# A subtraction one group earlier, a third chunk loaded into the result tile, and a reordered opening

## The chip, the cores and the metric

One core of one Trainium2 chip runs the whole program. The metric is the device time of one execution in microseconds (us); lower is better. Engines are named as in the profile: PE (TensorE matrix multiply), PEld (its weight load), DVE (VectorE), ACT (ScalarE), POOL (GpSimd), SP (the queue from which most transfers are issued).

## What is computed

The input is x (4 sequences of 4224 tokens with 192 channels). Three layers follow each other:

```python
# 1: a causal convolution of 7 taps, one softmax of the weights per head
out = np.einsum('hk,bskhg->bshg', w, x_unf)
# 2: rotation, mixing over all tokens, channel matrix
theta = x @ w_theta
zr = x * cos(theta);  zi = x * sin(theta)
y = einsum('ts,bsd->btd', w_tok_r, zr) + einsum('ts,bsd->btd', w_tok_i, zi)
u = x + y
x = u + np.maximum(u @ w_ch, 0.0)
# 3: low-rank token mixing (rank 32) and a two-layer channel network (192 -> 768 -> 192)
```

(In the reference z is formed from the convolved x; the kernel takes its rotated copy from the same theta product.) `w_tok_r` and `w_tok_i` are 4224 x 4224 each and stored in 64-bit floats, so they are most of what is loaded (308 MB are read in all).

## The kernel before

The mixing of layer 2 fills about three quarters of the run. Its result stays in one on-chip tile `yt` of six rows (`yt[:, j, :]`, j = 0 to 5: two pairs of sequences with three row blocks each) by 4224 token columns. Source tokens come in 33 blocks of 128. A **step** g (`mix_steps`, line 41) is one or two source blocks against one or two chunks of 512 target columns; each step has six **groups**, one per row j, and a group is 12 matmuls of 128x512 in the usual case (real and imaginary weights, and three products each: high by high, high by low, low by high, since each number is split into a rounded high part and the rest). `products` (line 764) issues them, `evict` (line 779) adds the sum from PSUM (the accumulator memory, four buffers `acc`) to `yt`. For the first source block evict copies on ACT (line 786) or, where told, on DVE (788); later it adds on DVE (784).

The weights of a step are two **pieces**, a = 2g (real) and b = 2g + 1 (imaginary). A piece goes through a chain: a transfer from SP into a raw buffer (`load_w`, line 394; a ring of two buffers `wraw`), unpacking of the 64-bit floats to 32 bits (`unpack_low` on ACT, line 278; `unpack_scale`, line 283 on ACT or 285 on DVE; `unpack_sign` 292 and `unpack_shift` 297 on DVE; the opening calls the last one "join"), the high part (ACT cast, line 703, into a ring of four tiles `w`), and the low part (subtraction, line 708, on DVE or POOL). The end of that subtraction frees the raw buffer and issues the transfer of the piece that follows in the ring (line 717). In the job lists below (piece, 0) is low and scale, (piece, 1) sign and shift, (piece, 2) the high part, (piece, 3) the subtraction.

`split_plan` (line 97) hands these jobs out by hand: list n of a step runs after the eviction of its group n. In a step of `TAILS` a **tail** (line 871: 128 more columns, with weights of their own) comes after group 3; lists 6 and 7 run within it, and lists 4 and 5 after groups 4 and 5. There are 15 such steps: the fourth step of each stage of eight steps from the third stage on (14 stages; stages 3 to 16, every 141.5 us) and step 10 in the second stage. There c is the first piece of the step after next.

Meanwhile the next source blocks are made in **units** (`prep_stages`, line 493): convolution (on DVE, lines 525 and 527, seven taps in two parts each, or on PE with diagonal matrices, line 537, then a copy by ACT, line 545), high and low parts (551; 573, 577, 581), theta (PE, lines 590 to 594), the reduction of the angle (617), sine and cosine, the rotation (635 and 638, "rot"), and high and low part of z (649 on ACT, "z_hi"; 652, "z_lo"), and `x_add` (658, on POOL), which adds the convolved x to `yt`. `unit_slots` plans them by group; the jobs of a list come before the unit's operations of the same group. In a tail step of the fourth stage and later, rot 1 and z_hi come at group 4, the first low/high casts of another unit (551) at group 5, its low parts (573 to 581) after group 0 of the next step, and its theta after group 2 of the next step.

The first three steps are written out by hand as the word list `OPENING` (line 65), which `open_mix` (795) executes in order: `W4.low` is a part of piece 4, `g1_3.0a` half a group of step 1 with row 3, `eg1_3.0` its eviction, `u0`, `u1`, `A`, `B` the first four units, `B.pc3` tap 3 of unit B on PE, `B.conva3` and `B.convb3` would be its two parts on DVE; `@dve` and `@pool` choose the engine. Each engine keeps the order of the words that are its own. Pieces 0 and 1 start in the ring, 2 and 3 in spare columns of `yt`; pieces 4 and 5 take the ring's buffers after pieces 0 and 1, and 6 and 7 after 4 and 5.

Of the kernel before, what the change touches and what calls it, by code (L numbers as in the profile page):

```python
# [12 lines left out]
I32 = mybir.dt.int32  # L13
# [5 lines left out]
P = 128  # L19
B, S, D = 4, 4224, 192  # L20
# [44 lines left out]
OPENING = """  # L65
    dg0.0 dg1.0 dg1.5 SL dg0.2 u0.pc0 dg1.1 dg1.6 dg0.1 dg0.5 dg1.4@act dg0.6@act dg0.4@act dg1.3@act dg0.3 dg1.2@act
    u0.pc1 u0.pc2 u0.pc3 u0.pc4 T.low u0.pc5 T.scale@dve T.sign W0.low u0.pc6 T.join T.t3 W1.scale T.t1 u1.pc0 W1.low
    u0.xhi2 T.t2@pool u1.pc1 W0.scale@dve T.t4@pool W0.sign W0.join u1.pc2 u0.xhi0@dve u0.xlo0 u0.xlo2 u0.xhi1 u1.pc3
    W1.sign u0.xcp u0.xlo1 W2.scale@dve W2.low W1.join u0.theta u1.pc4 W3.scale u0.turn0 W2.sign u0.turn1 W3.low
    W2.join u1.pc5 u1.pc6 u0.red0 u0.red1 u0.red2 u1.xhi2@dve u1.xhi0 W0.hi W1.hi u1.xhi1@dve u0.abs u1.xlo2 A.pc0  # L70
    u1.xlo0 u0.cos W0.lo@pool A.pc1 u1.xlo1 u0.rot0 W1.lo@pool A.pc2 u1.xcp A.pc3 A.pc4 A.pc5 A.pc6 u0.sin W3.sign
    u0.zhi0 A.xhi1 A.xhi2 A.xlo1 A.xlo2 A.xhi0 u0.zlo0@pool A.xcp u0.rot1 u1.theta u1.turn0 u0.zhi1 g0_0.0a u1.turn1
    u0.zlo1@pool W2.hi W3.join A.xlo0 u1.red0 g0_1.0a g0_2.0a A.theta g0_0.0 g0_1.0 u1.red1 u1.red2 W3.hi u1.abs
    eg0_0.0 W2.lo W3.lo u1.sin g0_2.0 A.turn0 eg0_1.0@dve eg0_2.0@dve u1.cos u1.rot0 A.xadd g1_0.0a u1.rot1 g1_0.1a
    g1_0.0 W4.low g1_0.1 u1.zhi0 g1_1.0a eg1_0.1 A.turn1@dve g1_1.1a u1.zhi1 eg1_0.0 u1.zlo0 g1_1.0 A.red0
    u1.zlo1@pool g1_1.1 g1_2.0a W5.low g1_2.1a g1_2.0 g1_2.1 B.pc0 eg1_1.1 eg1_1.0 B.pc1 W4.scale A.red1 g0_3.0a
    A.red2 g0_3.0 B.pc2 B.pc3 g0_4.0a eg1_2.0 eg1_2.1 A.abs g0_4.0 B.pc4 B.pc5 eg0_3.0 eg0_4.0 g0_5.0a g0_5.0 B.pc6
    B.xcp B.xhi2 B.xhi1 A.sin g1_3.0a W5.scale g1_3.0 B.xlo2 B.xhi0 g1_3.1a eg0_5.0 B.xlo1 B.xlo0 g1_3.1 g1_4.0a
    W4.sign W4.join eg1_3.0 W4.hi g1_4.0 W5.sign W5.join eg1_3.1 A.cos g1_4.1a W4.lo W5.hi A.rot0 g1_4.1 g1_5.0a
    g1_5.0 g1_5.1a W5.lo eg1_4.0 g1_5.1 eg1_4.1 A.zhi0 g2_0.0a g2_0.0 B.theta eg1_5.0 A.zlo0 W6.scale@dve W6.low  # L80
    eg1_5.1 A.rot1 B.turn0 W6.sign g2_1.0a g2_1.0 W6.join eg2_0.0 A.zhi1 B.turn1 W7.scale g2_2.0a g2_2.0 W7.low W6.hi
    eg2_1.0 B.red0 B.red1 B.red2 W7.sign eg2_2.0 g2_3.0a B.xadd B.abs W7.join A.zlo1 W6.lo g2_3.0 B.cos B.sin W7.hi
    B.rot0 g2_4.0a g2_4.0 eg2_3.0 B.zhi0 B.zlo0 W7.lo@pool eg2_4.0@dve B.rot1 W8.scale@dve W8.low B.zhi1 W8.sign
    g2_5.0a g2_5.0 B.zlo1 W8.join eg2_5.0 u1.xadd@dve u0.xadd@dve
""".split()
IDLE = 13
OPENED = 3
# [9 lines left out]
def split_plan():  # L97

    def following(g):
        return ("t", g + 1) if g + 1 in TAILS else 2 * (g + 2)  # L100

    plan = {}
    for g in range(OPENED, STARTS[-1]):
        a, b, c = 2 * (g + 1), 2 * (g + 1) + 1, following(g)
        if g in TAILS:
            t = ("t", g)
            jobs = [[(t, 2)], [(t, 3), (a, 0)], [(a, 1)], [(a, 2)], [(b, 2)], [(b, 3), (c, 0), (c, 1)]]
            jobs += [[(a, 3), (b, 0)], [(b, 1)]]
# [144 lines left out]
def mix_kernel(ctx, tc, xT, wcv, wth, wtok, wch, uu, vv, w1, w2, outT):  # L253
    nc = tc.nc
# [81 lines left out]
    with tc.manual_schedule():  # L336
# [27 lines left out]
        pieces = []  # L364
# [20 lines left out]
            ("t", g): (2 * kb, P, wu[:, 2 * s0 : 2 * (s0 + kb), TAIL:, :]) for g, (s0, kb) in TAILS.items()  # L385
        }
        stream = [0, 1]
        for h in range(4, len(pieces)):
            stream.append(h)
            if ("t", h // 2) in tails and h % 2:  # L390
                stream.append(("t", h // 2))
        follows = dict(zip(stream, stream[2:]))

        def load_w(h):
            if h not in tails and h >= len(pieces):
                return
# [19 lines left out]
        ident = cst.tile([P, P], F32, name="ident")  # L416
# [16 lines left out]
        def idle(n):  # L433
# [9 lines left out]
            out=wex, in0=wc_raw, in1=wmx.unsqueeze(2).to_broadcast([P, 2, TAPS]), op=ALU.subtract  # L443
# [9 lines left out]
            out=tap, in0=wex, in1=wsm.unsqueeze(2).to_broadcast([P, 2, TAPS]), op=ALU.mult  # L453
# [232 lines left out]
        def split_w(h, part, eng=None):  # L686

            tail = h in tails
            if part < 2:
                (unpack_parts, unpack_join)[part](raw[h])  # L690
                return
            src = words(raw[h], 1, F32)
            if tail:
                src = src.rearrange("p (u n) -> p u n", n=P)
                if h not in wt:
                    wt[h] = wp.tile([P, HALF], F32R, name="wtail", tag="w")
                hi = tail_part(h, 0)
            else:
                weight_tile(h // 2, h % 2)
                hi = weight_part(h // 2, h % 2, 0)  # L700
                src = src.rearrange("p (k n) -> p k n", k=pieces[h][0])
            if part == 2:
                nc.scalar.copy(hi, src)  # L703
            else:
                early = not tail and (h // 2 < STARTS[1] or h % 2 and h // 2 < STARTS[2]) and h != 2 * OPENED + 3
                eng = eng or (nc.gpsimd if early else nc.vector)
                lo = tail_part(h, 1) if tail else weight_part(h // 2, h % 2, 1)
                eng.tensor_tensor(out=lo, in0=src, in1=f(hi), op=ALU.subtract)  # L708
                del raw[h]
                late = 2 * STARTS[-1]  # L710
                if h == late - 1:
                    raw_st.close()
                    raws.update(pool=pool("wlate", bufs=2, stack=raw_st), n=2 * COLS)
                    load_w(late)
                    load_w(late + 1)
                elif h not in (2, 3, late - 2):
                    load_w(follows[h])


# [44 lines left out]
        def products(g, j, r, q):  # L764
            s0, kb, ranges = STEPS[g]
            if q == 0:
                sums[g, j, r] = ps_mm.tile([P, WMAX], F32, name="acc", tag="acc")[:, : ranges[r][1]]
            ps = sums[g, j, r]
            n, last = q * kb * 3, kb * 6 - 1
            high, low = weight_part(g, q, 0), weight_part(g, q, 1)  # L770
            for i in range(kb):
                z = zt[s0 + i]
                zh = z[:, q, j * P : (j + 1) * P]
                zl = z[:, 2 + q, j * P : (j + 1) * P]
                for a, b in ((zh, high), (zh, low), (zl, high)):
                    mm(ps, a, b[:, i + r, :], start=n == 0, stop=n == last)  # L776
                    n += 1
# [17 lines left out]
        def open_mix():  # L795
# [7 lines left out]
            for word in OPENING:  # L803
                word, _, eng = word.partition("@")
# [736 lines left out]
```

## Time and profile before

| what | value |
|---|---|
| median of 3 runs | 2968.41 us (2968.39 to 2968.72) |
| profiled execution | 2968.77 us, of which the span of instructions is 2967.0 us |
| PE busy | 2928.8 us (99%) |
| DVE busy | 2491.1 us (84%) |
| ACT busy | 1521.4 us (51%) |
| POOL busy | 365.9 us (12%) |
| mean granted TensorE clock | 0.999 of full speed |

Times inside the trace are microseconds from the span's start. A line of the order of time gives start, duration, engine, line of the kernel and operation, `out<-in`, the shape, and in brackets how long the engine had been idle before and what ended that.

### The profile page before, as it was taken

How to read it: one execution, taken by the hardware profiler on the slowest of the kernel's cores; microseconds unless marked ns; L12 is line 12 of the kernel's file. 1: busy time of each engine (PE TensorE's matmuls, PEld its weight loads, DVE VectorE, ACT ScalarE, POOL GpSimd, SP SyncE). 2: the span in 40 equal slices, each digit the busy share in tenths (PEclk: the TensorE clock that was granted, in tenths of full speed). 3: DMA queues.
4: the chain of work that ended last, by engine and by line, in shares of the span. 5: the costliest groups of instructions: out<-in, count | busy, mean ns of one | idle time of the engine just before them, and what ended most of it. 6: DMA issues, size and time to landing. Idle time of an engine off the chain costs nothing.

```text
span 2967.0 us, 37520 instructions
## 1 busy us (share of the span) xinstructions
PE 2928.8 (99%) x14284; PEld 2549.8 (86%) x14284; DVE 2491.1 (84%) x4003; ACT 1521.4 (51%) x2186; POOL 365.9 (12%) x269
## 2 busy tenths in 40 slices
PE   8999999999999999999999999999999999999999
PEld 7888888888888888888888888888889999999999
DVE  6899898989989898889898989888989887555555
ACT  6755555455555454554554555455446555444443
POOL 1221001111111111111111111111102211000000
PEclk9999999999999999999999999999999999999999
DMA  3433433343333343434333333334333221101110
GB/s 112 144 130 120 129 127 133 124 135 120 131 123 133 126 136 127 134 126 134 127 125 129 126 127 135 126 127 134 126 120 110 75 65 44 43 30 43 35 38 33
DMA packets 119013, 323.41 MB, mean 109 GB/s; under 512 B 6448, under 2 KB 48176, under 8 KB 117936
## 3 DMA queue, kind: packets, MB, share of 16 engines
q1 hardware_dynamic: 118432, 320.81, 32.7%
q8 instruction: 112, 1.84, 0.3%
q14 instruction: 69, 0.57, 0.1%
q10 hardware_dynamic: 400, 0.21, 0.0%
HBM read 308.01 MB, written 12.98 MB: 108 GB/s over the span
## 4 chain that ended last, share of the span: by engine, by line
PE 84%; DVE 11%; ACT 3%; issue 2%; DMA 1%; POOL 0%; ACTq 0%; DVEq 0%; POOLq 0%
PE acc L776 62%; DVE wraw L292 2%; DVE wraw L297 2%; DVE yt L784 2%; PE ob L1307 2%; PE acc L1269 2%; PE acc L1273 2%; PE oa L1309 2%; PE ob L1306 2%; PE oa L1311 2%; PE oa L1312 2%; PE acc L1270 2%; PE acc L1271 2%; PE acc L1272 1%; DVE xa L527 1%
## 5 line engine op out<-in xcount | busy, mean ns | idle before, releaser
L776 PE MATMUL acc<-w,z 128*128 128x512 f32 (+1 forms) x9720 | 2200.9, 386 | 26.5 <-DVE w L708 19.2
L776 PEld LDWEIGHTS acc<-w,z 128*128 128x128 f32 x9720 | 1805.2, 188 | 382.4 <-DVE w L708 26.2
L784 DVE TENSOR_TENSOR yt<-acc,yt 128x512 f32<-128x512 f32 (+1 forms) x786 | 527.4, 673 | 191.5 <-PE acc L776 187.1
L703 ACT CAST w<-wraw 128x1024 fp32r<-128x1024 f32 (+2 forms) x251 | 280.4, 1117 | 616.3 <-DVE wraw L297 610.3
L292 DVE TENSOR_SCALAR wraw<-wraw 128x1024 uint16<-128x1024 uint16 (+2 forms) x290 | 389.2, 1342 | 21.9 <-ACT wraw L283 13.8
L278 ACT ACTIVATE wraw<-wraw,consts 128x1024 int32<-128x1024 uint16 (+2 forms) x290 | 340.8, 1175 | 62.2 <-DMA wraw<-in_wtok 50.6
L297 DVE SCALAR_TENSOR_TENSOR wraw<-wraw 128x1024 int32<-128x1024 int32 (+2 forms) x290 | 358.3, 1236 | 9.3
L652 POOL TENSOR_TENSOR z<-tz,z 128x384 fp32r<-128x384 f32 x121 | 125.3, 1035 | 1777.3 <-ACT z L649 1749.5
L283 ACT ACTIVATE wraw<-wraw 128x1024 f32<-128x1024 f32 (+3 forms) x274 | 300.6, 1097 | 2.8 <-DMA wraw<-in_wtok 2.4
L527 DVE SCALAR_TENSOR_TENSOR xa<-xr,tap,xa 128x256 f32<-128x256 f32 x744 | 300.9, 445 | 0.0
L708 DVE TENSOR_TENSOR w<-wraw,w 128x1024 fp32r<-128x1024 f32 (+1 forms) x236 | 291.8, 1237 | 5.0 <-ACT w L703 5.0
L1281 DVE SCALAR_TENSOR_TENSOR hid<-acc,hid 128x384 fp32r<-128x384 f32 x264 | 146.7, 556 | 148.9 <-ACT hid L1278 148.0
L1278 ACT ACTIVATE hid<-acc 128x384 fp32r<-128x384 f32 x264 | 129.7, 492 | 250.1 <-PE acc L1273 233.9
L649 ACT CAST z<-tz 128x384 fp32r<-128x384 f32 x129 | 66.3, 514 | 297.9 <-DVE tz L638 297.9
L658 POOL TENSOR_TENSOR yt<-yt,xa 128x384 f32<-128x384 f32 x64 | 113.1, 1768 | 57.4 <-DVE xa L527 19.6
L1307 PE MATMUL ob<-hid,cl 128*128 128x384 f32 x264 | 89.2, 338 | 0.1
L1269 PE MATMUL acc<-fq,w 128*128 128x384 f32 x264 | 89.2, 338 | 0.0
L1273 PE MATMUL acc<-fq,w 128*128 128x384 f32 x264 | 89.0, 337 | 0.0
L1309 PE MATMUL oa<-hid,cl 128*128 128x384 f32 x264 | 88.7, 336 | 0.0
L1312 PE MATMUL oa<-hid,cl 128*128 128x384 f32 x264 | 88.7, 336 | 0.0
L1311 PE MATMUL oa<-hid,cl 128*128 128x384 f32 x264 | 88.7, 336 | 0.0
L1306 PE MATMUL ob<-hid,cl 128*128 128x384 f32 x264 | 88.6, 336 | 0.0
(249 smaller groups left out, 2876.0 us busy)
## 6 DMA issues: line engine op xcount, KB each, us to landing
wraw<-in_wtok SPq DMA_DIRECT2D x244, 1024.0 KB, 5.0
wraw<-in_wtok SPq DMA_DIRECT2D x23, 768.0 KB, 4.4
xr<-in_xT SPq DMA_DIRECT2D x63, 201.0 KB, 4.5
outT<-ot SPq DMA_DIRECT2D x20, 576.0 KB, 3.0
wraw<-in_wtok SPq DMA_DIRECT2D x18, 512.0 KB, 3.8
vzw<-in_vv SPq DMA_DIRECT2D x10, 384.0 KB, 4.1
wraw<-in_w SPq DMA_DIRECT2D x3, 768.0 KB, 4.2
yt<-in_wtok SPq DMA_DIRECT2D x2, 1024.0 KB, 9.3
```

The lines of the kernel that those rows point to most:

```text
L278: nc.scalar.activation(words(raw, 0), words(raw, 1, U16), AF.Identity, scale=2.0**-13, bias=consts[:, 3:4])
L283: nc.scalar.activation(w, w, AF.Copy, scale=2.0**-112)
L292: nc.vector.tensor_scalar(out=words(raw, 1, U16), in0=words(raw, 3, U16), scalar1=0x8000, scalar2=None, op0=ALU.bitwise_and)
L297: nc.vector.scalar_tensor_tensor(out=words(raw, 1), in0=words(raw, 1), scalar=3, in1=words(raw, 0), op0=ALU.logical_shift_left, op1=ALU.bi ...
L527: nc.vector.scalar_tensor_tensor(out=xa, in0=src, scalar=w, in1=xa, op0=ALU.mult, op1=ALU.add)
L703: nc.scalar.copy(hi, src)
L708: eng.tensor_tensor(out=lo, in0=src, in1=f(hi), op=ALU.subtract)
L776: mm(ps, a, b[:, i + r, :], start=n == 0, stop=n == last)
L784: nc.vector.tensor_tensor(out=dst, in0=ps, in1=dst, op=ALU.add)
L1269: mm(ps, w[0], q[:, b, :], start=True, stop=False)
L1273: mm(ps, w[3], q[:, 4 + b, :], start=False, stop=True)
L1307: mm(ob, c2[:, m, 2, :], h[:, 1, :], start=False, stop=last)
```

## The change

There are three parts.

1. In tail steps the subtraction of piece b, (b, 3), moves from list 5 to list 4, that is from behind group 5's eviction to behind group 4's. (b, 2), the ACT cast that it reads, stays in list 4 ahead of it.
2. Pieces 4 and 5 (step 2, the third pair) are loaded into columns 512 to 1535 of rows 5 and 4 of `yt`, by the words `d4 d5` behind `T.t4@pool`; a one-column POOL copy ahead of each transfer holds it back until then. The ring of two raw buffers goes from pieces 0 and 1 straight to 6 and 7, and after W4's and W5's subtractions nothing is loaded.
3. Unit B is convolved by DVE (`conva`, `convb`: 14 instructions) and no longer by PE (`pc0` to `pc6`), so its copy by ACT (`B.xcp`) goes; its convolved x lies in a spare place of `yt`. From there on the list has a new order: the scalings of pieces 4, 5 and 7 go from ACT to DVE, W4's subtraction from DVE to POOL, the unpacking of pieces 6 and 7 comes ahead of step 2, and piece 8's four unpacking words stand at the very end, behind the two last `x_add`.

```diff
@@ OPENING
-    u0.xhi2 T.t2@pool u1.pc1 W0.scale@dve T.t4@pool W0.sign W0.join u1.pc2 u0.xhi0@dve u0.xlo0 u0.xlo2 u0.xhi1 u1.pc3
+    u0.xhi2 T.t2@pool u1.pc1 W0.scale@dve T.t4@pool d4 d5 W0.sign W0.join u1.pc2 u0.xhi0@dve u0.xlo0 u0.xlo2 u0.xhi1
...
-    g1_0.0 W4.low g1_0.1 u1.zhi0 g1_1.0a eg1_0.1 A.turn1@dve g1_1.1a u1.zhi1 eg1_0.0 u1.zlo0 g1_1.0 A.red0
-    u1.zlo1@pool g1_1.1 g1_2.0a W5.low g1_2.1a g1_2.0 g1_2.1 B.pc0 eg1_1.1 eg1_1.0 B.pc1 W4.scale A.red1 g0_3.0a
-    A.red2 g0_3.0 B.pc2 B.pc3 g0_4.0a eg1_2.0 eg1_2.1 A.abs g0_4.0 B.pc4 B.pc5 eg0_3.0 eg0_4.0 g0_5.0a g0_5.0 B.pc6
-    B.xcp B.xhi2 B.xhi1 A.sin g1_3.0a W5.scale g1_3.0 B.xlo2 B.xhi0 g1_3.1a eg0_5.0 B.xlo1 B.xlo0 g1_3.1 g1_4.0a
-    W4.sign W4.join eg1_3.0 W4.hi g1_4.0 W5.sign W5.join eg1_3.1 A.cos g1_4.1a W4.lo W5.hi A.rot0 g1_4.1 g1_5.0a
-    g1_5.0 g1_5.1a W5.lo eg1_4.0 g1_5.1 eg1_4.1 A.zhi0 g2_0.0a g2_0.0 B.theta eg1_5.0 A.zlo0 W6.scale@dve W6.low
-    eg1_5.1 A.rot1 B.turn0 W6.sign g2_1.0a g2_1.0 W6.join eg2_0.0 A.zhi1 B.turn1 W7.scale g2_2.0a g2_2.0 W7.low W6.hi
-    eg2_1.0 B.red0 B.red1 B.red2 W7.sign eg2_2.0 g2_3.0a B.xadd B.abs W7.join A.zlo1 W6.lo g2_3.0 B.cos B.sin W7.hi
-    B.rot0 g2_4.0a g2_4.0 eg2_3.0 B.zhi0 B.zlo0 W7.lo@pool eg2_4.0@dve B.rot1 W8.scale@dve W8.low B.zhi1 W8.sign
-    g2_5.0a g2_5.0 B.zlo1 W8.join eg2_5.0 u1.xadd@dve u0.xadd@dve
+    g1_0.1a g1_0.0 g1_0.1 u1.zhi0 W4.low g1_1.0a eg1_0.1 A.turn1@dve g1_1.1a u1.zhi1 eg1_0.0 u1.zlo0 g1_1.0 A.red0
+    u1.zlo1@pool g1_1.1 g1_2.0a W5.low g1_2.1a g1_2.0 g1_2.1 A.red1 A.red2 g0_3.0a eg1_1.1 eg1_1.0 g0_3.0 A.abs
+    B.convb0 B.convb1 B.convb2 eg1_2.0 B.convb3 eg1_2.1 B.convb4 B.convb5 B.convb6 A.cos A.sin g0_4.0a g0_4.0 B.xhi2
+    B.xhi1 B.conva0 B.conva1 eg0_3.0 B.conva2 B.conva3 g0_5.0a g0_5.0 B.conva4 B.conva5 B.conva6 eg0_4.0 B.xhi0
+    W4.scale@dve W4.sign W4.join B.xlo2 B.xlo1 g1_3.0a g1_3.0 eg0_5.0 W4.hi B.xlo0 A.rot0 W5.scale@dve W5.sign W5.join
+    A.zhi0 W5.hi g1_3.1a g1_3.1 B.theta W4.lo@pool eg1_3.0 A.zlo0 A.rot1 g1_4.0a g1_4.0 W5.lo W6.low eg1_3.1 A.zhi1
+    B.turn0 W6.scale@dve W6.sign B.turn1 g1_4.1a g1_4.1 A.zlo1 W6.join eg1_4.0 B.red0 B.red1 B.red2 g1_5.0a g1_5.0
+    W7.low eg1_4.1 B.abs W7.scale@dve W7.sign B.cos g1_5.1a g1_5.1 B.sin W7.join eg1_5.0 B.rot0 g2_0.0a g2_0.0 eg1_5.1
+    W6.hi B.zhi0 B.zlo0 W6.lo g2_1.0a g2_1.0 eg2_0.0 W7.hi B.rot1 g2_2.0a g2_2.0 eg2_1.0 W7.lo@pool B.zhi1 B.xadd
+    B.zlo1 eg2_2.0@dve g2_3.0a g2_3.0 g2_4.0a g2_4.0 eg2_3.0 g2_5.0a g2_5.0 eg2_4.0 eg2_5.0 u1.xadd@dve u0.xadd@dve
+    W8.scale@dve W8.low W8.sign W8.join
@@ split_plan
-            jobs = [[(t, 2)], [(t, 3), (a, 0)], [(a, 1)], [(a, 2)], [(b, 2)], [(b, 3), (c, 0), (c, 1)]]
+            jobs = [[(t, 2)], [(t, 3), (a, 0)], [(a, 1)], [(a, 2)], [(b, 2), (b, 3)], [(c, 0), (c, 1)]]
@@ stream and load_w
-        for h in range(4, len(pieces)):
+        for h in range(6, len(pieces)):
...
+            elif h in (4, 5):
+                t = spare(9 - h, 512, 2 * WMAX).bitcast(I32).rearrange("p (n w) -> p n w", w=2)
+                nc.gpsimd.tensor_copy(out=spare(9 - h, 512, 1), in_=ident[:, 0:1])
@@ conv_tiles
+                    elif (i, p) == (1, 1):
+                        st["xa"] = spare(3, 2060, 3 * P).rearrange("p (j s) -> p j s", j=3)
@@ split_w
-                elif h not in (2, 3, late - 2):
+                elif h in follows and h != late - 2:
                     load_w(follows[h])
@@ open_mix
+                elif word in ("d4", "d5"):
+                    load_w(int(word[1]))
```

## Rows read from the trace of the kernel before

**Rows 1.** The longest wait of PE: engine, line, releaser: us, times, longest.
```profile
PE acc L776 <- DVE w L708: 19.2, 16, 1.3
```

**Rows 2.** PE in order of time at the first and last tail step's end.
```profile
330.55 9.59 PE L776 MATMUL acc<-w,z 128*128 128x512 f32 x41 [1.31 <-DVE w L708]
...
2170.32 1.42 PE L776 MATMUL acc<-w,z 128*128 128x512 f32 x5 [1.20 <-DVE w L708]
```

**Rows 3.** All engines in order of time around one of them, 467 to 479 us.
```profile
467.27 1.14 ACT L703 CAST w<-wraw 128x1024 fp32r<-128x1024 f32 x1 [2.35 <-DVE wraw L297]
...
468.82 0.41 DVE L635 TENSOR_TENSOR tz<-th,ta 128x256 f32<-128x256 f32 x1
...
470.00 0.68 DVE L784 TENSOR_TENSOR yt<-acc,yt 128x512 f32<-128x512 f32 x1
470.05 1.01 POOL L652 TENSOR_TENSOR z<-tz,z 128x384 fp32r<-128x384 f32 x1 [7.61 <-ACT z L649]
470.60 1.55 DVE L708 TENSOR_TENSOR w<-wraw,w 128x1024 fp32r<-128x1024 f32 x1
471.00 1.23 ACT L283 ACTIVATE wraw<-wraw 128x1024 f32<-128x1024 f32 x1
471.03 1.99 POOL L658 TENSOR_TENSOR yt<-yt,xa 128x384 f32<-128x384 f32 x1
...
472.21 6.87 PE L776 MATMUL acc<-w,z 128*128 128x512 f32 x29 [1.23 <-DVE w L708]
472.26 1.97 DVE L292 TENSOR_SCALAR wraw<-wraw 128x1024 uint16<-128x1024 uint16 x1
...
476.77 0.29 DVE L581 TENSOR_TENSOR xq<-xa,xq 64x128 fp32r<-64x128 f32 x1
...
478.91 0.30 PE L590 MATMUL th<-t,xq 128*128 128x320 f32 x1
```

**Rows 4.** Groups by line and shape, 472.21 to 613.69 us: count | busy, mean ns | idle before.
```profile
L784 DVE TENSOR_TENSOR yt<-acc,yt 128x512 f32<-128x512 f32 x48 | 32.8, 684 | 12.0 <-PE acc L776 11.9
L708 DVE TENSOR_TENSOR w<-wraw,w 128x1024 fp32r<-128x1024 f32 x16 | 19.8, 1234 | 0.4 <-ACT w L703 0.4
L527 DVE SCALAR_TENSOR_TENSOR xa<-xr,tap,xa 128x256 f32<-128x256 f32 x24 | 12.3, 514 | 0.0
```

**Rows 5.** PE in order of time in the opening, 59 to 92 us.
```profile
63.01 3.02 PE L776 MATMUL acc<-w,z 128*128 128x512 f32 x12 [0.23 <-ACT yt L786]
68.53 1.88 PE L776 MATMUL acc<-w,z 128*128 128x512 f32 x7 [2.50 <-ACT yt L786]
71.23 1.67 PE L776 MATMUL acc<-w,z 128*128 128x512 f32 x6 [0.82 <-DVE w L708]
74.03 16.61 PE L776 MATMUL acc<-w,z 128*128 128x512 f32 x72 [1.13 <-POOL w L708]
91.84 0.50 PE L776 MATMUL acc<-w,z 128*128 128x512 f32 x1 [1.19 <-DVE w L708]
```

**Rows 6.** Unit B's taps on PE (line 537): sum over their four stretches.
```profile
sum 4.27, PE 4.26 PEld 3.86; mean PE 1.06 PEld 0.97
```

**Rows 7.** ACT in order of time: its waits for pieces 6 and 8.
```profile
61.22 1.27 ACT L278 ACTIVATE wraw<-wraw,consts 128x1024 int32<-128x1024 uint16 x1 [3.09 <-DMA wraw<-in_wtok]
...
76.42 1.27 ACT L278 ACTIVATE wraw<-wraw,consts 128x1024 int32<-128x1024 uint16 x1 [4.06 <-DMA wraw<-in_wtok]
```

**Rows 8.** SP in order of time: issues of weight transfers.
```profile
21.88 1.61 SPq L406 DMA_DIRECT2D wraw<-in_wtok  x2
...
56.04 28.67 SPq L406 DMA_DIRECT2D wraw<-in_wtok  x5
```

**Rows 9.** DVE in order of time in the opening: an idle stretch, a slow operation.
```profile
49.92 0.29 DVE L581 TENSOR_TENSOR xq<-acc,xq 64x128 fp32r<-64x128 f32 x1 [13.85 <-ACT xq L551]
...
72.40 1.99 DVE L652 TENSOR_TENSOR z<-tz,z 128x384 fp32r<-128x384 f32 x1 [0.69 <-ACT z L649]
```

**Rows 10.** Busy time of all engines, 39.86 to 70.20 us.
```profile
sum 30.34, PE 27.48 PEld 22.12 DVE 15.28 ACT 18.49 POOL 1.01; mean PE 13.74 PEld 11.06 DVE 7.64 ACT 9.25 POOL 0.51
```

More of the change, by code (lines that the diff above doesn't have):

```diff
@@ L67 @@
     u0.pc1 u0.pc2 u0.pc3 u0.pc4 T.low u0.pc5 T.scale@dve T.sign W0.low u0.pc6 T.join T.t3 W1.scale T.t1 u1.pc0 W1.low
-    u0.xhi2 T.t2@pool u1.pc1 W0.scale@dve T.t4@pool W0.sign W0.join u1.pc2 u0.xhi0@dve u0.xlo0 u0.xlo2 u0.xhi1 u1.pc3
-    W1.sign u0.xcp u0.xlo1 W2.scale@dve W2.low W1.join u0.theta u1.pc4 W3.scale u0.turn0 W2.sign u0.turn1 W3.low
-    W2.join u1.pc5 u1.pc6 u0.red0 u0.red1 u0.red2 u1.xhi2@dve u1.xhi0 W0.hi W1.hi u1.xhi1@dve u0.abs u1.xlo2 A.pc0
-    u1.xlo0 u0.cos W0.lo@pool A.pc1 u1.xlo1 u0.rot0 W1.lo@pool A.pc2 u1.xcp A.pc3 A.pc4 A.pc5 A.pc6 u0.sin W3.sign
@@ L72 @@
-    u0.zhi0 A.xhi1 A.xhi2 A.xlo1 A.xlo2 A.xhi0 u0.zlo0@pool A.xcp u0.rot1 u1.theta u1.turn0 u0.zhi1 g0_0.0a u1.turn1
-    u0.zlo1@pool W2.hi W3.join A.xlo0 u1.red0 g0_1.0a g0_2.0a A.theta g0_0.0 g0_1.0 u1.red1 u1.red2 W3.hi u1.abs
-    eg0_0.0 W2.lo W3.lo u1.sin g0_2.0 A.turn0 eg0_1.0@dve eg0_2.0@dve u1.cos u1.rot0 A.xadd g1_0.0a u1.rot1 g1_0.1a
-    g1_0.0 W4.low g1_0.1 u1.zhi0 g1_1.0a eg1_0.1 A.turn1@dve g1_1.1a u1.zhi1 eg1_0.0 u1.zlo0 g1_1.0 A.red0
-    u1.zlo1@pool g1_1.1 g1_2.0a W5.low g1_2.1a g1_2.0 g1_2.1 B.pc0 eg1_1.1 eg1_1.0 B.pc1 W4.scale A.red1 g0_3.0a
@@ L82 @@
-    eg2_1.0 B.red0 B.red1 B.red2 W7.sign eg2_2.0 g2_3.0a B.xadd B.abs W7.join A.zlo1 W6.lo g2_3.0 B.cos B.sin W7.hi
-    B.rot0 g2_4.0a g2_4.0 eg2_3.0 B.zhi0 B.zlo0 W7.lo@pool eg2_4.0@dve B.rot1 W8.scale@dve W8.low B.zhi1 W8.sign
-    g2_5.0a g2_5.0 B.zlo1 W8.join eg2_5.0 u1.xadd@dve u0.xadd@dve
+    u0.xhi2 T.t2@pool u1.pc1 W0.scale@dve T.t4@pool d4 d5 W0.sign W0.join u1.pc2 u0.xhi0@dve u0.xlo0 u0.xlo2 u0.xhi1
+    u1.pc3 W1.sign u0.xcp u0.xlo1 W2.scale@dve W2.low W1.join u0.theta u1.pc4 W3.scale u0.turn0 W2.sign u0.turn1
@@ new lines @@
+    W3.low W2.join u1.pc5 u1.pc6 u0.red0 u0.red1 u0.red2 u1.xhi2@dve u1.xhi0 W0.hi W1.hi u1.xhi1@dve u0.abs u1.xlo2
+    A.pc0 u1.xlo0 u0.cos W0.lo@pool A.pc1 u1.xlo1 u0.rot0 W1.lo@pool A.pc2 u1.xcp A.pc3 A.pc4 A.pc5 A.pc6 u0.sin
+    W3.sign u0.zhi0 A.xhi1 A.xhi2 A.xlo1 A.xlo2 A.xhi0 u0.zlo0@pool A.xcp u0.rot1 u1.theta u1.turn0 u0.zhi1 g0_0.0a
+    u1.turn1 u0.zlo1@pool W2.hi W3.join A.xlo0 u1.red0 g0_1.0a g0_2.0a A.theta g0_0.0 g0_1.0 u1.red1 u1.red2 W3.hi
+    u1.abs eg0_0.0 W2.lo W3.lo u1.sin g0_2.0 A.turn0 eg0_1.0@dve eg0_2.0@dve u1.cos u1.rot0 A.xadd g1_0.0a u1.rot1
```

## The prediction

> **What bounds the kernel now.** I read the page first: PE is busy 99% of the span, so a gain must come from PE work that goes away or from the few stretches in which PE stands still. The list of waits comes second [rows 1]: 19.2 us of PE's idle time is its wait for weight subtractions on DVE, 16 times, never over 1.3 us. PE's own order of time says where: 14 of the 16 recur every 141.5 us, from 330.55 to 2170.32 [rows 2], always in the first group of the step after a tail step; the other two (0.82 and 1.19) lie in the opening [rows 5]. So the tails cost 19.2 - 0.82 - 1.19 = 17.2 us, about 1.23 each. Third, the opening: between 63 and 92 us PE stands still for 0.23 + 2.50 + 0.82 + 1.13 + 1.19 = 5.87 us [rows 5]. DVE is not the bound in a steady stage: in 141.5 us it waits 11.9 us for PE sums to evict [rows 4].
>
> **Part 1, the moved subtraction.** In the order of all engines at one tail step [rows 3], the cast that it reads ends at 467.27 + 1.14 = 468.41. DVE is through with group 4's eviction at 468.82, where the rotation starts. Then come the rotation, two tap operations and group 5's eviction (470.00), and only at 470.60 the subtraction, which takes 1.55. PE had come to it at 472.21 - 1.23 = 470.98. Put behind group 4's eviction it starts at 468.82 without a wait for its cast, and takes 1.23, the mean of its kind [rows 4], so it ends near 470.05; with the 1.55 seen, at 470.4. PE needs it at 470.98: the whole stall goes, 14 x 1.23 = 17.2 us at most. The transfer that its end issues on SP comes earlier too; nothing stands against that.
>
> What is queued behind it on DVE: the rotation (whose result ACT casts before it unpacks the next piece c), the last tap, group 5's eviction, the sign pass of c, the first eviction of the next step, and the three low parts of a unit, whose theta product stands in PE's queue. Rotation, cast and c's scaling move by about 1.1: the scaling, ended at 472.23, ends near 473.4, and the sign pass (472.26 before) starts there. That pass took 1.97 beside `x_add` on POOL (1.99). With DVE idle for a moment ahead of it, `x_add`, which follows POOL's subtraction of z (1.01 for the same size) at about 472.2, should be nearly done by then, and the pass nearer to the 1.3 left when the overlap of 0.7 is taken off. The low parts, ended at 477.06, would end near 477.4 in that case, and near 478.2 if the overlap stays. Theta started on PE at 478.91 [rows 3]; with PE 1.23 earlier it is called at 477.68. So the next thing late is theta, by 0 to 0.5 us. I take 0.1, since the sign pass will start after most of `x_add`: **1.1 us a stage, 14 x 1.1 = 15.5 us**, ends 14 x 0.7 = 10 and 17.2. What is left of the delay on DVE disappears in its 11.9 us of waits per stage [rows 4].
>
> The tail of step 10 has its subtraction on POOL and no stall behind it. A POOL subtraction moved by a group can block DVE elsewhere: the nearest row is the 384-column subtraction that took 1.99 at 72.40, where a free one should need about 0.5, three quarters of a 512-column eviction [rows 4, 9]. I take 0 and keep +-1.5 us.
>
> **Part 2, the third pair of weights.** Before, pieces 4 and 5 took the ring at 21.88, and piece 6 could be issued only at 56.04, behind piece 4's subtraction [rows 8]. ACT then stood idle 3.09 us for it until 61.22, with evictions behind it in its queue [rows 7]; this holds PE's sum buffers, and gives the 0.23 and the 2.50. Pieces 6 and 7, late from the start, give the 0.82 and 1.13, and piece 9, behind piece 8 that lands at 76.42 [rows 7], the 1.19. Now 6 and 7 take the ring at 21.88; a megabyte was in use 61.22 - 56.04 = 5.2 us after its issue, so both lie ready some 20 us before they are unpacked. The two earlier transfers of half that size ride behind pieces 2 and 3 on SP, with no issue behind them until 21.88 [rows 8]; if they slowed pieces 2 and 3 by sharing, that would cost PE at most 5.2, still inside the range below. Pieces 2 and 3 were issued first, so I take 0. The one-column copies sit on POOL ahead of subtractions that have not begun.
>
> **Part 3, unit B and the order.** PE loses the B taps: 4.27 us, start to start [rows 6], at full clock. DVE gets 14 tap operations, at most 0.514 each [rows 4] = 7.2, and three scalings, at most a subtraction of 1.23 each = 3.7; it loses W4's subtraction. It was busy 15.28 of the 30.34 us from 39.86 to 70.20 [rows 10], and idle 13.85 on end until 49.92 [rows 9], so from 36.07; the taps now go there. Is it in time? PE asked for piece 6's low part at 71.23 - 0.82 = 70.41 [rows 5]; without the taps and the first two stalls that is 70.41 - 4.27 - 2.73 = 63.4. From 36.07 to 63.4 are 27.3 us, the work at most 15.28 + 7.2 + 3.7 = 26.2. It fits, without much to spare in the worst case. Piece 8 is issued when piece 6 is split, so between 60 and 63.4, and lands 5.2 later, at 65 to 68.6. Piece 9's low part came 91.84 - 76.42 = 15.4 after piece 8's landing, so it comes at 80.6 to 84.0; it will be called at 91.84 - 1.19 - 4.27 - 0.23 - 2.50 - 0.82 - 1.13 = 81.7. So this stall lies between 0 and 2.3; I take 0, as the two `x_add` no longer stand between. **Opening: 4.27 + 5.87 = 10.1 us**, ends 10.5 and, with 0.82, 1.13 and 2.3 not gained, 10.1 - 0.82 - 1.13 - 2.3 = 5.9.
>
> One row speaks against this part: 1.99 for a DVE subtraction while POOL worked at a 1024-column one [rows 9]. W4's subtraction now runs on POOL beside DVE's unpacking, and W7's beside W6's. The Trainium skill has a rule for it (SBUF — State Buffer, Who interferes with whom): a DVE instruction with two SBUF inputs and a GpSimd instruction that reads SBUF contend, and the second to issue blocks fully until the first is done. The row agrees as far as it goes. It is the mechanism of rival B.
>
> **Sum.** Profiled execution 2968.77 - 15.5 - 10.1 = 2943.2. The median lies 0.36 under the profiled execution, so 2942.8: **2943 us**, 0.86% faster. Its own range is 2939 to 2947.
>
> **Rivals.**
> A. *Theta takes the stall's place.* The sign pass keeps its 1.97 and the low parts end at 478.2: 0.5 of the 1.2 comes back, 14 x 0.7 = 9.8. For it: the overlap is there in the trace; against it: `x_add` will start against an idle DVE. Time 2968.4 - 9.8 - 10.1 = 2948.5.
> B. *Opening given back.* DVE, blocked behind POOL subtractions, is late for pieces 6, 7 and 9. For it: the 1.99; against: the idle 13.85. Opening 5.9: 2968.4 - 15.5 - 5.9 = 2947.
> C. *Part 1 does nothing.* The cast or the subtraction comes late after all, for example by a wait for a free tile of `w`, and the stall stays. Against it: the cast ended 0.4 before DVE was free. Time 2968.4 - 10.1 = 2958.3.
> D. *Slower.* The three low parts slip further than the moved instruction, and PE waits at theta in each of 14 stages. If they slip by S, PE waits S - 0.62 there (478.91 - 477.06 - 1.23 = 0.62); a stage loses from S = 1.85, the whole is back at the old time at S = 2.54 and 5.9 us slower from 2.96. With 1.55 for the subtraction, 0.65 for the sign pass and 1.4 for a low part blocked as at 72.40, S is 3.6 at most; at 3.3 the time is 2968.4 + 14 x 1.45 - 10.1 = 2978.6. Against it: I work out 0.3 to 1.1.
>
> **How the numbers follow.** Forecast 0.50, A 0.17, B 0.15, C 0.08, better than 2939 (the small eviction waits near 233 to 252 us or step 10 gain too) 0.03, D with S between 2.1 and 2.96 0.03, D beyond 0.04. The range runs from 2938 to 2954: forecast, A, B and their sum; C and D are left out. A measurement of this kernel can tell about 0.2% (5.9 us) from no change. Faster 0.50 + 0.17 + 0.15 + 0.08 + 0.03 = 0.93, same 0.03, slower 0.04.
>
> **What would show it.** Part 1 is right if the idle time of line 776 behind DVE's line 708 falls from 19.2 to under 2 us, the 14 rows at the stages' starts are gone, and a stage takes 140.3 to 140.4 in place of 141.5. A shows as idle time of PE at lines 590 to 592 behind DVE lines 573 to 581, 14 times. C leaves the 14 rows as they are. Part 2 is right if SP issues four weight transfers of the ring and the spare place before 25 us, and ACT no longer waits 3.09 for a transfer near 60. Part 3 is right if DVE's gap of 13.85 is filled and step 4 begins near 80 to 82 us rather than at 90; B shows as waits of PE for line 708 there. The prediction is wrong if PE's idle time in the first 100 us does not fall by at least 3.

## The result and the profile after

The changed kernel takes **2939.7 us** in the median (2939.08 to 2941.12, 4 runs) against 2968.56 (2968.39 to 2969.51, 4 runs): ratio 0.9903, 95% interval 0.9886 to 0.9920, 28.9 us less. In a second session beside other runs of the kernel before it was 2940.29 against 2968.48. The profiled execution of the changed kernel took 2939.08 us with a span of 2937.3, 29.7 less than the span before. The time lies inside the forecast's range; the gain was foreseen at 25.6 us, so 3.3 too small.

PE's waits in the changed kernel, the list of waits (engine, line, releaser: us, times, longest). Line 782 was 776, 714 was 708, 790 was 784, 792 was 786:

```profile
PE acc L782 <- DVE yt L790: 2.9, 4, 1.0
...
PE acc L782 <- ACT yt L792: 1.1, 2, 0.9
...
PE th L597 <- DVE xq L579: 0.5, 1, 0.5
```

The 19.2 us behind the weight subtractions [rows 1] are gone altogether: no row of PE behind line 714 is left, neither from the tails nor from the opening. The 2.73 behind ACT's evictions [rows 5] are 1.1.

A tail step's end in the order of all engines, the place of [rows 3]:

```profile
452.57 13.80 PE L782 MATMUL acc<-w,z 128*128 128x512 f32 x60
...
456.11 1.14 ACT L709 CAST w<-wraw 128x1024 fp32r<-128x1024 f32 x1 [2.34 <-DVE wraw L298]
...
457.06 0.69 DVE L790 TENSOR_TENSOR yt<-acc,yt 128x512 f32<-128x512 f32 x1
457.66 1.22 DVE L714 TENSOR_TENSOR w<-wraw,w 128x1024 fp32r<-128x1024 f32 x1
458.79 0.42 DVE L641 TENSOR_TENSOR tz<-th,ta 128x256 f32<-128x256 f32 x1
...
459.98 0.69 DVE L790 TENSOR_TENSOR yt<-acc,yt 128x512 f32<-128x512 f32 x1
...
460.99 1.14 ACT L284 ACTIVATE wraw<-wraw 128x1024 f32<-128x1024 f32 x1
461.02 1.02 POOL L664 TENSOR_TENSOR yt<-yt,xa 128x384 f32<-128x384 f32 x1
...
462.16 1.34 DVE L293 TENSOR_SCALAR wraw<-wraw 128x1024 uint16<-128x1024 uint16 x1 [1.49 <-ACT wraw L284]
...
466.04 0.29 DVE L587 TENSOR_TENSOR xq<-xa,xq 64x128 fp32r<-64x128 f32 x1
466.21 0.30 PE L596 MATMUL th<-t,xq 128*128 128x320 f32 x1
```

The subtraction (457.66) follows group 4's eviction without a wait and takes 1.22 (it was 1.55). `x_add` on POOL takes 1.02 (1.99), the sign pass 1.34 (1.97), after DVE has idled 1.49 for ACT. PE runs its 60 matmuls from 452.57 to theta without a break.

The opening on PE, in order of time, the place of [rows 5]:

```profile
53.90 3.27 PE L782 MATMUL acc<-w,z 128*128 128x512 f32 x12 [0.16 <-ACT yt L792]
58.12 27.69 PE L782 MATMUL acc<-w,z 128*128 128x512 f32 x120 [0.94 <-ACT yt L792]
```

Of five waits (5.87 us) two are left (1.10). The 120 matmuls from 58.12 run through step 3 and into step 4 without a stop.

The transfers of pieces 4 and 5, then of 6 and 7 (SP in order of time):

```profile
12.16 0.82 SPq L410 DMA_DIRECT2D yt<-in_wtok  x2
22.12 1.64 SPq L410 DMA_DIRECT2D wraw<-in_wtok  x2
```

ACT's first word on piece 6, which waited 3.09 us for its data before [rows 7], now comes without a wait:

```profile
50.10 1.27 ACT L279 ACTIVATE wraw<-wraw,consts 128x1024 int32<-128x1024 uint16 x1
```

Unit B's taps fill DVE's gap of 13.85 [rows 9]: they run from 36.19 to 42.95.

**Where the 29.7 us come from.** Landmarks of the two traces, set side by side (start times of PE operations, own subtraction):

| landmark | before | after | gained so far |
|---|---|---|---|
| a theta in the first stage | 121.65 | 111.43 | 10.22 |
| tail of step 10 | 206.95 | 196.63 | 10.32 |
| a theta at the end of the second stage | 271.72 | 262.12 | 9.60 |
| tail of the third stage | 317.85 | 308.25 | 9.60 |
| last tail | 2157.73 | 2128.25 | 29.48 |
| first transposes after it | 2171.58 | 2140.61 | 30.97 |
| next theta | 2177.75 | 2148.07 | 29.68 |

The opening gives 10.2; 0.7 of it is lost in the second stage. Thirteen stage ends give 29.48 - 9.60 = 19.88, that is 1.53 each, and the fourteenth 1.49. A wait that was not there before takes 1.3 back right after the last tail. A stage takes 140.0 us ((2128.25 - 308.25) / 13) in place of 141.5.

### The profile page after: what moved, and what is told of

Read it like the earlier page. It is cut to its first block, busy times and chain, and to the rows that moved or that the text cites. A ratio compares the mean times of both kernels' runs of the same rounds, so it can differ in the third digit from the quotient of the medians.

```text
span 2937.3 us, 37483 instructions
## 1 busy us (share of the span) xinstructions
PE 2919.9 (99%) x14256; PEld 2548.0 (87%) x14256; DVE 2486.9 (85%) x4019; ACT 1518.8 (52%) x2182; POOL 358.5 (12%) x272
## 4 chain that ended last, share of the span: by engine, by line
PE 90%; DVE 6%; ACT 1%; issue 1%; DMA 1%; POOL 0%; SPq 0%; ACTq 0%; DVEq 0%; POOLq 0%
PE acc L782 68%; PE acc L877 2%; PE ob L1315 2%; PE acc L1281 2%; PE acc L1277 2%; PE oa L1317 2%; PE ob L1314 2%; PE oa L1320 2%; PE oa L1319 2%; PE acc L1278 2%; PE acc L1279 2%; PE acc L1280 2%; DVE yt L790 1%; DVE wraw L293 1%; DVE wraw L298 1%
## 5 line engine op out<-in xcount | busy, mean ns | idle before, releaser
L293 DVE TENSOR_SCALAR wraw<-wraw 128x1024 uint16<-128x1024 uint16 (+2 forms) x288 | 381.5, 1325 | 40.5 <-ACT wraw L284 34.4
L664 POOL TENSOR_TENSOR yt<-yt,xa 128x384 f32<-128x384 f32 x63 | 102.4, 1626 | 40.9 <-DVE xa L533 18.5
```

The lines of the kernel that those rows point to most:

```text
L293: nc.vector.tensor_scalar(out=words(raw, 1, U16), in0=words(raw, 3, U16), scalar1=0x8000, scalar2=None, op0=ALU.bitwise_and)
```

## The experiments

Each kernel was timed beside runs of the kernel before on the same chip; the gain is against the median of those (2968.16 for e1 to e4, 2967.66 for e5 to e8, 2968.48 for e9 and the changed kernel again; each of the three groups ran on a chip of its own).

| kernel | median us | gain us |
|---|---|---|
| tails alone (e1) | 2947.6 | 20.6 |
| opening alone (e2) | 2960.09 | 8.1 |
| ring alone (e3) | 2966.89 | 1.3 |
| taps and order (e4) | 2962.01 | 6.2 |
| taps alone (e7) | 2962.26 | 5.4 |
| taps and ring (e9) | 2962.57 | 5.9 |
| changed, subtraction twice (e5) | 2951.28 | 16.4 |
| changed, one eviction earlier (e6) | 2939.7 | 28.0 |
| changed, one subtraction off POOL (e8) | 2938.97 | 28.7 |
| changed, again | 2940.29 | 28.2 |

**Tails alone.** The kernel before with one line changed:

```diff
-[(b, 2)], [(b, 3), (c, 0), (c, 1)]]
+[(b, 2), (b, 3)], [(c, 0), (c, 1)]]
```

> The kernel before with the moved subtraction alone; opening and ring as before. Theory H (a stall costs more than the idle time shown, because the matmul record ahead of it already covers part of the gap: 1.52 us each, as 60 matmuls over one such place took 15.16 us before and 13.64 after): 14 x 1.52 = 21.3, less 1.3 for the new wait in the last tail stage, so about 2948.5 us. Theory I (the idle time shown is the whole cost, 1.23 each, as predicted): 17.2 less 1.0, about 2952.3. Rival, the two parts help each other: clearly above 2952.

Measured 2947.6: theory H. Taking 14 rows of 1.2 us away gives 20.6 us, not 17. In the trace the 14 rows are gone, and the new wait after the last tail (PE in order of time) is there without any change to the opening:

```profile
2154.34 3.02 PE L776 MATMUL acc<-w,z 128*128 128x512 f32 x12 [1.08 <-DVE yt L784]
```

**Opening alone.** The changed kernel with the old job line put back.

> The changed kernel with the old job list of the tail steps: the opening and the ring alone. The 14 stalls of 1.2 us come back as rows. If the parts add: 2968.5 - 10.2 = 2958.3 us, and the difference to the changed kernel is 18.6 to 20 us under theory H (14 x 1.52 less the last stage's new wait), 16.2 under theory I (then 2956).

Measured 2960.09, 20.4 above the changed kernel: again theory H (a little more than its 18.6 to 20). The time itself misses the 2958.3 by 1.8, because less of the opening's gain is kept than the first 111 us show. The rows of PE at the stages' starts are back, 14 times and 17.4 us in the list of waits:

```profile
463.37 6.91 PE L782 MATMUL acc<-w,z 128*128 128x512 f32 x29 [1.22 <-DVE w L714]
```

The two halves add up: 20.6 + 8.1 = 28.7 against 28.9 and 28.2 for both. The opening is worth 8.1 over the whole run, although this kernel's trace is 10.15 ahead at the first stage's landmark (111.50 against 121.65) and 8.83 at the second stage's end (262.89 against 271.72): 1.3 is given back there.

**Ring alone.** In the kernel before, `d4 d5`, the stream from 6 and the condition for the next load are changed as in the diff; taps, order and tails are not.

> The kernel before with pieces 4 and 5 loaded into the result tile and the ring skipped to 6 and 7; word order, unit B on PE and tails as before. Theory ring (the waits of PE from 63 to 92 us come from piece 6's late transfer): ACT's 3.09 us wait near 60 goes, and with it most of the 5.87 us, so 4 to 6.5 us faster, 2962 to 2964.5. Rival, the order (DVE and ACT reach the words of pieces 6 and 7 late anyway): under 2 us faster, above 2966.5.

Measured 1.3 us: the rival. PE in order of time:

```profile
57.98 1.66 PE L779 MATMUL acc<-w,z 128*128 128x512 f32 x6 [0.50 <-ACT yt L789]
66.66 1.88 PE L779 MATMUL acc<-w,z 128*128 128x512 f32 x7 [0.26 <-ACT yt L789]
69.38 1.67 PE L779 MATMUL acc<-w,z 128*128 128x512 f32 x6 [0.84 <-DVE w L711]
72.16 16.66 PE L779 MATMUL acc<-w,z 128*128 128x512 f32 x72 [1.11 <-POOL w L711]
89.69 4.15 PE L779 MATMUL acc<-w,z 128*128 128x512 f32 x17 [0.88 <-DVE w L711]
```

The 2.50 behind ACT's eviction shrinks to 0.26, since ACT no longer waits 3.09 for piece 6 [rows 7]; a new wait of 0.50 stands at 57.98. But the waits for the subtractions of pieces 6, 7 and 9 stay at 0.84, 1.11 and 0.88 (before 0.82, 1.13 and 1.19 [rows 5]): the data is there early, and the words that unpack it still stand late in each engine's list. ACT starts on piece 6 without a wait for data, but at 59.20 (61.22 before, 50.10 in the changed kernel):

```profile
59.20 1.28 ACT L278 ACTIVATE wraw<-wraw,consts 128x1024 int32<-128x1024 uint16 x1
```

**Taps and order, ring as before.** The changed kernel without `d4 d5`, with the old stream and the old tails.

> The new word order with unit B on DVE, but pieces 4 and 5 take the ring as before and the tails are the old ones. Theory ring: piece 6 is issued behind piece 4's subtraction, now near 47 us, and lands near 52; ACT and DVE wait 2 to 4 us in their queues, part of the stalls stays: gain 4.3 (the taps) to 7, 2961.5 to 2964. Rival, the order alone does it: gain 9 to 10.2, 2958.3 to 2959.5.

Measured 6.2: theory ring. Three of the subtractions' waits are gone, but ACT waits 2.06 us for piece 6 ahead of evictions, and PE 2.13 behind those; ACT, then PE, in order of time:

```profile
52.41 1.25 ACT L279 ACTIVATE wraw<-wraw,consts 128x1024 int32<-128x1024 uint16 x1 [2.06 <-DMA wraw<-in_wtok]
```

```profile
54.19 5.97 PE L779 MATMUL acc<-w,z 128*128 128x512 f32 x18 [2.13 <-ACT yt L789]
60.40 27.71 PE L779 MATMUL acc<-w,z 128*128 128x512 f32 x120 [0.24 <-ACT yt L789]
```

**Taps alone.** The kernel before with unit B's 14 tap operations on DVE behind `A.red2`, and its PE taps and `B.xcp` gone (its convolved x lies in the spare place, as in the change; lists shortened):

```diff
-A.red1 g0_3.0a A.red2 g0_3.0 B.pc2 B.pc3 g0_4.0a
+A.red1 g0_3.0a A.red2 B.convb0 ... B.convb6 B.conva0 ... B.conva6 g0_3.0 g0_4.0a
...
-B.pc6 B.xcp B.xhi2
+B.xhi2
```

> The kernel before with unit B's taps on DVE, put behind A.red2, and B.xcp gone; ring, other word order and tails as before. If the taps are path: ACT no longer waits 2.83 us for them near 48.9, everything behind shifts, 4 to 4.5 us faster, 2964. Rival, the stretch to step 4 is bound by the chain of pieces 4, 6 and 8, not by PE: PE arrives early and waits longer, gain under 2 us, above 2966.5.

Measured 5.4, more than the taps' 4.27 [rows 6] and than the 4 to 4.5 expected: they were on the path. Between the same two points on PE, from the 105 matmuls ahead of unit B's theta to the first one behind it, this trace needs 25.11 us (28.74 to 53.85) and the one before 30.24 (29.58 to 59.82), so 5.1 goes with the taps' 4.27. The waits behind them stay in kind (1.75, 0.82, 1.14 and 0.75 in its trace; before 2.50, 0.82, 1.13 and 1.19). ACT still waits 2.98 for piece 6, now at 53.93.

**Taps and ring, old order.** Both edits together.

> Unit B's taps on DVE behind A.red2 and the ring skipped to pieces 6 and 7, both in the old word order with the old tails: what is left to the new order is the difference to the opening-only kernel (2960.1). Theory 'taps and ring, the order adds little' (the order with taps alone gave 6.2, the taps alone 5.4): 6.5 to 8 us faster than before, 2960 to 2961.5. Theory 'order' (the words of pieces 6 and 7 stand late in the old list, so 0.82, 1.13 and 0.8 stay): 5.4 to 6.5 faster, above 2961.5, with those rows.

Measured 5.9, theory 'order': with 0.86, 1.07 and 1.09 at the three subtractions in its trace. So the ring adds 0.5 to the taps, the order (with the words that change their engine) adds 0.8, and both together 2.7 (8.1 - 5.4). Each is worth little without the other: early data needs early words, and early words need early data. These steps of 0.5 and 0.8 are near what the runs scatter (1 to 3 us within one kernel), the 2.7 is not. The traces order them the same way: from the matmuls behind unit A's theta (near 29 us) to the theta at the first stage's landmark PE needs 85.1 us with the taps alone, 84.7 with taps and order, 84.0 with taps and ring, 82.6 with all three (92.1 before).

**Subtraction twice.** The changed kernel, in the 14 tail steps:

```diff
+                if not tail and h % 2 and h // 2 - 1 in TAILS and h // 2 > STARTS[2]:
+                    eng.tensor_tensor(out=lo, in0=src, in1=f(hi), op=ALU.subtract)
                 eng.tensor_tensor(out=lo, in0=src, in1=f(hi), op=ALU.subtract)
```

> The changed kernel with the moved subtraction done twice in the 14 tail steps of stages 3 to 16 (same result, 1.13 us more of DVE in that place). Theory theta (rival D's mechanism): in the changed kernel the low parts end 0.12 us after theta's first product starts, and the product that needs the second of them has about 0.6 us to spare; 1.13 more makes PE wait about 0.55 there, 0.8 with the hidden part of a stall, in most of the 14 stages: 2948 to 2952 us, with rows of PE waiting at lines 597 to 600. By the prediction's own formula (slip 1.58 less 0.62 is 0.96 a stage) 2953. Rival, DVE's spare time takes it up before theta is called: no change, 2940.

The size is as theory theta said (11.6 us over the first median of the changed kernel, 0.8 a stage), the place is not. PE waits at the old place, the first group of the step; theta's products show no row of waiting. All engines in order of time:

```profile
460.74 1.22 DVE L716 TENSOR_TENSOR w<-wraw,w 128x1024 fp32r<-128x1024 f32 x1
...
462.02 6.89 PE L784 MATMUL acc<-w,z 128*128 128x512 f32 x29 [0.34 <-DVE w L716]
...
468.75 0.30 PE L596 MATMUL th<-t,xq 128*128 128x320 f32 x1
```

1.25 us more in that place makes the low part 0.34 late, so the moved subtraction had about 0.9 to spare. From the tail (450.29) to theta (468.75) this kernel needs 18.46 us, the changed one 466.21 - 448.41 = 17.80: a wait shown as 0.34 costs 0.66. Theta's products lose a little too: from theta to the next mixing product it is 1.33 (468.75 to 470.08), before the doubling 1.24 (466.21 to 467.45). Together that is 0.75 a stage, and with the wait after the last tail, 1.63 in place of 1.03, it makes 11.1 us.

**One eviction earlier.** In the changed kernel's opening:

```diff
-B.abs W7.scale@dve ... W7.join eg1_5.0 B.rot0
+eg1_5.0 B.abs W7.scale@dve ... W7.join B.rot0
```

> The changed kernel with the word eg1_5.0 moved ahead of B.abs in the opening, so that ACT evicts that sum before it waits for the reductions. If the 0.94 us wait of PE at 58.12 comes from this eviction: the row goes, 0.9 to 1.25 us faster, 2938.5; if another buffer is the last one, the wait stays and nothing changes, 2939.7.

No change. The wait of 0.94 leaves 58.12 and a wait of 0.91 stands one buffer on; PE in order of time:

```profile
60.71 24.96 PE L782 MATMUL acc<-w,z 128*128 128x512 f32 x108 [0.91 <-ACT yt L792]
```

That one eviction is not the bound; ACT as a whole seems to be behind in this stretch.

**One subtraction off POOL.** In the changed kernel, piece 25 (step 12):

```diff
-early = ... and h != 2 * OPENED + 3
+early = ... and h not in (2 * OPENED + 3, 2 * STARTS[2] - 1)
```

> The changed kernel with one subtraction, that of step 12's second piece, on DVE and not on POOL. In the changed kernel a low part of a unit beside it takes 2.45 us in place of 0.29 and the next 0.98, and theta and the sums behind wait. If the two engines block each other there: those two go back to 0.3, DVE pays 1.13, PE's waits of 0.24 and 0.99 at 228 and 243 us shrink, 0.7 to 2 us faster, 2938 to 2939. Rival, DVE is simply full there: its own 1.13 more costs as much, 2939.7 to 2941.

2938.97: in the range of the block, but with no difference to the changed kernel (2939.7 and 2940.29) that the scatter of 1 to 2 us would let stand. What is shown is the block itself. DVE and POOL in order of time, first the changed kernel, then this one:

```profile
223.58 2.52 POOL L714 TENSOR_TENSOR w<-wraw,w 128x1024 fp32r<-128x1024 f32 x1 [4.05 <-issue]
223.80 2.45 DVE L583 TENSOR_TENSOR xq<-xa,xq 64x128 fp32r<-64x128 f32 x1
...
226.28 0.98 DVE L587 TENSOR_TENSOR xq<-xa,xq 64x128 fp32r<-64x128 f32 x1
```

```profile
224.93 0.29 DVE L583 TENSOR_TENSOR xq<-xa,xq 64x128 fp32r<-64x128 f32 x1
225.25 0.29 DVE L587 TENSOR_TENSOR xq<-xa,xq 64x128 fp32r<-64x128 f32 x1
```

A 0.29 us operation takes 2.45 beside POOL's subtraction and ends with it. Without it, a sum's eviction is late by more (1.31 in place of 0.58 at 224 us) and others by less: DVE is nearly full there either way.

## Why the prediction was right, and where its terms were off

**The sum was closer than its terms.** The tails were forecast at 15.5 and gave 20.6 alone; the opening was forecast at 10.1 and gave 8.1 alone. One term was 5.1 too small and the other 2.0 too large, so part of the sum's closeness is luck. Two slips of arithmetic change nothing: 14 x 1.1 is 15.4, and rival D's limits should be 2.57 and 2.99 for 2.54 and 2.96.

**Part 1: mechanism right, size too small.** The steps came as worked out: the cast was there, the subtraction ran unblocked in 1.22, `x_add` ran against an idle DVE in 1.02, the sign pass fell to 1.34, and the three low parts ended 0.12 us after theta began (466.33 against 466.21) without a row of PE waiting. Rival A, and D with it, did not come: the low parts slipped by 0.45 in place of 0.34 (1.85 to spare before, -0.12 now, and theta 1.52 earlier). The term that was mis-sized is the price of a stall. I took the idle time shown, 1.23, and 0.1 off. The 60 matmuls from a tail to theta took 478.91 - 463.75 = 15.16 us before and 466.21 - 452.57 = 13.64 after, 1.52 less. This is the row of the kernel before ahead of the stall, with [rows 3]:

```profile
463.75 7.22 PE L776 MATMUL acc<-w,z 128*128 128x512 f32 x31
```

The matmuls start every 0.227 us (13.64 / 60), but a record lasts 386 ns in the mean, as the page's costliest group of the changed kernel says (busy, mean ns of one | idle before):

```profile
L782 PE MATMUL acc<-w,z 128*128 128x512 f32 (+1 forms) x9720 | 2194.9, 386 | 5.6 <-DVE yt L790 2.9
```

So the last record before a wait covers 0.16 us of it and counts as busy, and the first record after a wait is 0.11 longer, 0.50 at 91.84 [rows 5]. Together that is 0.27 of the 0.29 that the row does not show. The run of tails alone (20.6), the difference with and without them (20.4) and the doubled subtraction (0.34 shown, 0.66 paid) agree on it. At 1.52 a stage the term would have been 21.3, less the wait after the last tail; a stage takes 140.0 us, not the 140.3 to 140.4 of the prediction.

**That wait** (1.03 at 2145.22 in the changed kernel's trace, 1.08 with the tails alone) I did not foresee. In the last of these stages two transposes take sum buffers right behind the tail step, and DVE, 1.49 idle for ACT ahead of the sign pass, evicts the first group too late for them. It is the delay of about 1.1 us on ACT that part 1 of the prediction had worked out, but it shows at a sum buffer and once, not at theta and 14 times. Step 10's moved subtraction cost nothing, as taken: with the tails alone, tail to theta of that stage takes 64.77 us as before.

**Parts 2 and 3: the sum right at 111 us, one step wrong.** The forecast was 10.1; the traces differ by 10.2 there. Step 4 was forecast to begin at 80 to 82; 24 + 72 matmuls behind 58.12 at 0.2293, start to start (27.52 us to the next theta at 85.64, over 120), put it at 80.1. Piece 8 was forecast to land at 65 to 68.6; ACT's wait for it ends at 67.10. Over the whole run the opening is worth 8.1, since 0.7 (changed kernel) to 1.3 (opening alone) is lost again near 200 to 262 us. The forecast has no term for this: its +-1.5 was for step 10's moved subtraction, and the loss is there with the old tails too. The wrong step is the cause of three stalls: I put 0.82, 1.13 and 1.19 down to the transfers of pieces 6, 7 and 9 coming late. With early transfers alone they stay (0.84, 1.11, 0.88); they go only when the words are moved too. The price of the waits came out nearly right because the change makes both moves; with the cause misread, that is luck.

**Rival B** did not come as it was put: no row of PE waits behind line 714 in the opening. But POOL's subtraction of piece 4 does hold DVE up. The scaling of piece 5 takes 1.01 beside it; the same scaling of piece 4, without POOL at work, took 0.42 at 42.87:

```profile
45.72 1.44 POOL L714 TENSOR_TENSOR w<-yt,w 128x512 fp32r<-128x512 f32 x1 [8.57 <-ACT w L709]
46.44 1.01 DVE L286 TENSOR_SCALAR yt<-yt 128x512 f32<-128x512 f32 x1
```

DVE then works without a break until the reductions for which ACT waits 0.54 at 56.00, ahead of the evictions behind PE's wait at 58.12. Whether the 0.59 is a part of that wait was not tested. The rule that I had cited from the Trainium skill (SBUF — State Buffer, Who interferes with whom), that the second of the two engines to issue blocks until the first is done, fits the 2.45 at 223.80, which ends 0.15 after POOL's operation. **Rival C** fell with the cast at 456.11 to 457.25, ahead of DVE's 457.66.

**Where the second stage loses.** From the tail of step 10 to the theta at the stage's end it takes 64.77 us before, 65.49 in the changed kernel, 66.11 with the opening alone. The 0.7 lies at one theta, whose low parts stand beside the same subtraction on POOL in both kernels: before, it holds up the last of the three, in the changed kernel the second. From this theta to the next mixing product it is 1.58 before (236.07 to 237.65), 2.28 after (225.76 to 228.04). The kernel before, all engines in order of time (the changed kernel's POOL and DVE rows stand above, at 223.58):

```profile
234.27 2.45 POOL L708 TENSOR_TENSOR w<-wraw,w 128x1024 fp32r<-128x1024 f32 x1 [4.43 <-issue]
234.44 2.43 DVE L581 TENSOR_TENSOR xq<-xa,xq 64x128 fp32r<-64x128 f32 x1
```

The changed kernel, PE and its weight load in order of time: theta's fourth product comes when the second low part is done, its ninth when the third is.

```profile
226.30 0.19 PEld L599 LDWEIGHTS th<-t,xq 128*128 128x128 f32 x1 [0.20 <-DVE xq L583]
226.30 0.39 PE L599 MATMUL th<-t,xq 128*128 128x256 f32 x1
...
227.31 0.19 PEld L599 LDWEIGHTS th<-t,xq 128*128 128x128 f32 x1 [0.34 <-DVE xq L587]
227.31 0.39 PE L599 MATMUL th<-t,xq 128*128 128x256 f32 x1
...
228.04 13.90 PE L782 MATMUL acc<-w,z 128*128 128x512 f32 x60 [0.24 <-DVE yt L790]
```

Without the block (e8) it is 1.24 from this theta to the next mixing product, but PE waits longer ahead of it (0.83 and 1.31, at 214 and 224 us), so the run gains nothing. The further 0.6 of the opening alone goes with a wait of 0.48 at 214.58 that the changed kernel's trace does not have; the five traces with such a wait between 214 and 217 us need 65.9 to 66.6 from the tail to the stage's last theta, the seven without it 64.8 to 65.6. **Left open** is why the subtraction falls one low part earlier, and where that last wait comes from.

## What to carry to other kernels

Price a stall of a pipelined engine by the time from start to start over the same work, with and without it, not by the idle time of the row: here each wait of 1.2 us cost 1.5, and one of 0.34 cost 0.66. When work on a full engine comes late for its reader, look first at what stands ahead of it in that engine's own order: one subtraction put ahead of 1.8 us of work that could wait took away a stall that came back 14 times. Early data and an early place in the engine's list are two conditions; an edit that meets one of them may gain next to nothing.

## What was not expected of the hardware

The granted TensorE clock falls, in some profiles, after PE's two waits near 23 to 25 us (0.61 and 0.96 in the kernel before). From 27 to 30 us it is 0.60 to 0.80 in six of the twelve profiles and 1.00 in the other six. In this stretch, busy time by engine and the granted clock (after POOL), the changed kernel and the one with the earlier eviction:

```profile
27.00:30.00 3.00, 3.00 (x14) 2.71 (x14) 2.84 (x5) 2.86 (x4) 0.91 (x1) 0.62 0.92 344
```

```profile
27.00:30.00 3.00, 2.98 (x18) 2.42 (x17) 2.83 (x6) 3.00 (x6) 1.01 (x1) 1.00 0.94 361
```

A mean of 0.62 lies between the two levels, 1.2 and 2.4 GHz (0.5 and 1.00), so most of that stretch ran at the lower one. The waits are the same in both (0.66 and 0.95; 0.61 and 0.94), so what tips it is not in these rows. The seven matmuls from 25 us then take 2.90 in place of 1.89. In the changed opening little of that is left later: from the first product (23.59 and 23.79) to the theta at 111 us it is 87.84 and 87.50, 0.34 apart. Two more kernels with the changed opening show the same: 87.54 (opening alone) and 87.51 (one subtraction off POOL) at a clock of 1.00, and the changed kernel once more, whose clock fell again (0.80), 88.00. PE waits for ACT's evictions in both kernels above (0.16 and 0.94 us near 54 and 58; 0.35 and 0.91 near 54 and 61), so ACT is the likely bound that takes the rest back; no run tests that.
